# B and C a round sooner, decay rows two blocks ahead, the wide sums earlier in four steps, VectorE's operand ahead of ScalarE's

## The chip, the core and the metric

The kernel runs on one core of a Trainium2 chip, beside whose TensorE (PE) work the vector engine (DVE), the scalar engine (ACT) and GpSimd (POOL); SyncE (SP) issues the DMAs. The metric is device time in microseconds for one execution, smaller is better.

## The reference: what is computed

A chunked linear attention with decay feeds two layers without a residual between them, all in 32-bit floats:

```python
log_a = np.log(np.clip(a, 1e-06, 1.0))      # batch 4, 8 heads, 768 rows
cum = np.cumsum(la, axis=-1)                # within a chunk
L = np.exp(cum[:, :, :, None] - cum[:, :, None, :]) * causal
CB = np.einsum('bhin,bhjn->bhij', Cc, Bc)   # d_state 16
y_intra = np.einsum('bhij,bhjd->bhid', CB * L, xc)          # head_dim 32
y_inter = np.einsum('bhin,bhnd->bhid', Cc, state) * np.exp(cum)[:, :, :, None]
state = decay_full * state + np.sum(Bx * decay_from_j, axis=2)
...
x = attention as 3072 x 256
h = np.maximum(np.maximum(x @ w1, x @ w2), x @ w3)          # 256 -> 768
x = h @ w_out                                               # 768 -> 256
h = x @ w_in                                                # 256 -> 2048
g = np.maximum(h, 0.0) + alpha * np.minimum(h, 0.0)
out = g @ w_out                                             # 2048 -> 256
```

The chunk length only divides the work: another length gives the same values.

## The kernel before

**Tiles.** The 4 x 768 tokens are 24 blocks r of 128 rows, six to a batch element. Four blocks make a tile t of 512 tokens; the layers run over tiles. Each layer matrix product is three products: weights and activations are split into a high and a low part (`w`: high and low; `gh`, `gl`: the high and low part of an intermediate; `xt`: those of the attention's output). All the three-product matmuls are issued at L640 (`up<-xt,w` and `acc<-gh,wo` and `acc<-gl,wo` in the rows); `halves` makes `gh` on ACT (L131) and `gl` on POOL (L132). Weights arrive as 64-bit words (`st`) and are converted by ACT L164, DVE L171 and L173, ACT L177, DVE L179.

**One attention block.** `load` asks for B, C and x; `att_a` scales B and C by their decays on POOL (`bp`, `cp`, L345); `att_t` transposes B, C and `cp` on PE (L386), ACT copies `cpt` (L389), ACT makes C's operand `cs` with two copies (L394) and DVE B's operand `bs` with one multiplication (L395), both in one tile `bc`; `att_b` forms C B^T (PE L464) and multiplies it by the decays `e` (DVE L469); `att_e` makes these decays: `cum_rows` has asked for rows of cumulative sums over a DMA (L336, into `e`), ACT exponentiates them head by head (L442, eight a block) and POOL clears what is not causal (L445, two selects a block); `att_u` makes the new state (PE L497, DVE L503 and L509) and asks for the next block's rows; `att_y` forms the output (PE L538 from the state, PE L546 from `e` and x) into `xt` (ACT L555, DVE L556). Blocks 0 to 11 work in two chunks of 64 rows ("direct"), blocks 12 to 23 in one of 128 ("wide"); the wide ones use other row sums (`cum_w`), made by `wide_sums` and `wide_back` once, out of PE (L308, L313, L319), ACT (L309, L315, L320) and DVE (L314, L322).

**What sets the order.** The first 20.5 us (blocks 0 and 1 of the attention) stand in an order written by hand. Then layer 1 on tile 0 runs, in units of 256 tokens, and the attention blocks 2 and on are cut into steps on a list `todo`, of which a quota is handed out between units; within this first phase (to 84 us) the instructions are ordered by a scheduler that goes by its own estimates, afterwards (`STRICT`) again as written. SP issues all DMAs in order; each waits for the landing of the one issued eight before. Readers and writers of one tile run in the order in which they are written.

The lines that the change touches sit in this place of the program:

```python
        todo += rounds(2)
        for i, go in enumerate((lambda: wide_sums(0), lambda: wide_sums(1), wide_back)):
            todo.insert(WIDE + 3 * i, (go, 0))
```

`NB` is 6 blocks a batch element, `NR` 24, `NDIR` the first wide block (12), `NPA` (2) the first block whose rows come by DMA.

Of the kernel before, what the change touches and what calls it, by code (L numbers as in the profile page):

```python
# [41 lines left out]
AHEAD = 8  # L42
# [10 lines left out]
WIDE = 18  # L53
ORDER = [(0, 0), (1, 0), (0, 1), (1, 1), (2, 0), (2, 1)]
BW = 2
# [24 lines left out]
def fused(ctx: ExitStack, tc: tile.TileContext, x, a, B, C, w1, w2, w3, w_out, v_in, v_out, alpha, cst, out):  # L80
# [11 lines left out]
    NDIR = BW * NB  # L92
# [121 lines left out]
    def load(r):  # L214
        for q in (r, r + 1)[r > AHEAD:1 + (r >= AHEAD)]:
            load_bc(q)
        load_x(r)
# [84 lines left out]
    def wide_sums(half):  # L302

        ks = slice(3 * half, 3 * half + 3)
        cols = slice(3 * P * half, 3 * P * (half + 1))
        pc = ptile(ps_at, "at", (BT * H, 3 * P))
        for k in range(3):
            nc.tensor.matmul(pc[:, k * P:(k + 1) * P], s_la[:, 3 * half + k, :], s_c[:, C_TW:C_TW + P], start=True, stop=True)  # L308
        nc.scalar.activation(s_a[:, cols], pc, AF.Copy)  # L309
        nc.sync.dma_start(cum_w[:, cols], s_a[:, cols])  # L310
        pt = ptile(ps_at, "at", (P, 3, BT, H))
        for k in range(3):
            nc.tensor.transpose(pt[:, k].rearrange("p b h -> p (b h)"), s_a[:, (3 * half + k) * P:(3 * half + k + 1) * P], ident[:BT * H, :BT * H])  # L313
        nc.vector.tensor_scalar(ncum[:, ks, BW:, :], pt[:, :, BW:, :], -1.0, None, ALU.mult)  # L314
        nc.scalar.activation(dec_c[:, ks, BW:, :], pt[:, :, BW:, :], AF.Exp)  # L315

    def wide_back():
        pd = ptile(ps_at, "at", (P, NB, BT, H))
        nc.tensor.matmul(pd.rearrange("p k b h -> p (k b h)"), s_c[:, C_TW + P:C_SEL], s_la.rearrange("p k h -> p (k h)"), start=True, stop=True)  # L319
        nc.scalar.activation(dec_b[:, :, BW:, :], pd[:, :, BW:, :], AF.Exp)  # L320
        half = dec_f[:, BW:, :].rearrange("p b (k c) -> p b k c", c=2)
        nc.vector.tensor_tensor(dec_w.unsqueeze(3), half[:, :, :, 0:1], half[:, :, :, 1:2], ALU.mult)  # L322

    def cum_rows(r):
        b, k = divmod(r, NB)
        d = blk.setdefault(r, {})
        if r >= NDIR:
            for g in range(2):
                e = d["m", g] = em.tile([P, 4, P], F32, tag="e", name="e")
                src = cum_w[b * H + 4 * g:b * H + 4 * g + 4, k * P:(k + 1) * P]  # L330
                nc.sync.dma_start(e, src.unsqueeze(0).to_broadcast([P, 4, P]))
            return
        e = d["m"] = em.tile([P, H, Q], F32, tag="e", name="e")
        for c in range(2 if r >= NPA else 0):
            src = cum_d[2 * k + c, b * H:(b + 1) * H, :]
            nc.sync.dma_start(e[c * Q:(c + 1) * Q], src.unsqueeze(0).to_broadcast([Q, H, Q]))  # L336

# [32 lines left out]
    def att_t(r, part=None):  # L370
# [19 lines left out]
        if "b" in keys:  # L390
            bc = stk.tile([P, 6, P], F32R, tag="bc", name="bc").bitcast(F32)
            bs, cs = d["bs"], d["cs"] = bc[:, :2], bc[:, 2:4]
            for i in range(2):
                nc.scalar.activation(cs[:, i, :], pt[:, 1, :], AF.Copy, scale=par[i])  # L394
            nc.vector.tensor_tensor(bs, pt[:, 0:1, :].to_broadcast([P, 2, P]), pairs.to_broadcast([P, 2, P]), ALU.mult)  # L395
# [78 lines left out]
    def att_u(r):  # L474
        b, k = divmod(r, NB)
        d = blk[r]
        if r >= NDIR:
# [14 lines left out]
            if r + 1 < NR:  # L492
                cum_rows(r + 1)
# [17 lines left out]
        if 0 < r < NR - 1:  # L511
            cum_rows(r + 1)
# [239 lines left out]
    with tc.manual_schedule():  # L752
# [52 lines left out]
        next_weights(START)  # L805
    load(2)
    if True:
# [8 lines left out]
        for i, go in enumerate((lambda: wide_sums(0), lambda: wide_sums(1), wide_back)):  # L816
            todo.insert(WIDE + 3 * i, (go, 0))
# [82 lines left out]
```

## Time and profile before

| quantity | value |
|---|---|
| median of 3 runs | 549.5 us (549.48 to 550.97) |
| the profiled execution's own time | 548.96 us |
| its span in the trace | 547.2 us |
| granted PE clock, mean over the span | 0.995 |

The profile is of the one execution whose time is 548.96 us: the span leaves 1.76 us outside it. Times below are microseconds from the span's start. A granted clock of 1.00 is TensorE's upper level of 2.4 GHz, 0.50 its lower level of 1.2 GHz, and what lies between is a stretch that had both.

### The profile page before, as it was taken

The page shows a single profiled execution, that of the slowest core. Times are in us where ns is not written, and L with a number is a line of the kernel's source. Part 1 is how long each engine was busy: PE and PEld are TensorE (multiplying, and loading weights), DVE is VectorE, ACT ScalarE, POOL GpSimd, SP SyncE. Part 2 cuts the span into 40 slices and gives each one's busy share as a digit, 9 for nine tenths or more (in the row PEclk, how much of TensorE's full clock was granted, in tenths as well). Part 3 has the DMA queues.
Part 4 walks back from the last instruction along what each step waited for, and adds up shares of the span by engine and source line. Part 5 has one row for each costly group of instructions (what it writes and reads, how often), then busy time and mean ns, then how long its engine had stood idle before and what let it go on. Part 6 is the DMA issues. An engine that isn't in the chain of part 4 may idle for free.

```text
span 547.2 us, 9715 instructions
## 1 busy us (share of the span) xinstructions
PE 536.1 (98%) x3541; PEld 434.4 (79%) x3542; DVE 333.0 (61%) x592; ACT 223.1 (41%) x556; POOL 224.9 (41%) x251
## 2 busy tenths in 40 slices
PE   8899999999999999999999999999999999999997
PEld 4678887787887888888788888888877888888885
DVE  5887886868995446764437665346654336556553
ACT  5667766654634325244242423424242223222222
POOL 2143443423746325464233654324453213444441
PEclk9998999999999999999999999999999999999999
DMA  7978797433635546253743544744210200002001
GB/s 144 235 147 185 184 184 175 125 97 116 140 73 127 89 104 137 53 121 73 140 87 72 121 86 81 130 86 113 56 41 2 38 1 0 1 0 40 0 2 39
DMA packets 185632, 49.84 MB, mean 91 GB/s; under 512 B 144112, under 2 KB 177072, under 8 KB 185584
## 3 DMA queue, kind: packets, MB, share of 16 engines
q1 hardware_dynamic: 185584, 49.22, 42.2%
q8 instruction: 28, 0.46, 0.4%
q14 instruction: 20, 0.16, 0.1%
HBM read 40.48 MB, written 8.72 MB: 90 GB/s over the span
## 4 chain that ended last, share of the span: by engine, by line
PE 87%; DMA 4%; DVE 3%; ACT 3%; issue 1%; SPq 1%; POOL 0%; ACTq 0%; DVEq 0%; POOLq 0%
PE up L640 48%; PE acc L640 31%; PE at L525 1%; DMA st<-in_moe_w_out_dram 1%; PE at L454 1%; DMA e<-cum_d 1%; DMA b<-in_B_dram 1%; DMA st<-in_moe_w_in_dram 1%; PE at L546 1%; PE at L464 1%; ACT e L442 1%; PE at L522 1%; PE up L750 1%; PE at L538 1%; DVE v L173 0%
## 5 line engine op out<-in xcount | busy, mean ns | idle before, releaser
L132 POOL TENSOR_TENSOR gl<-g,gh 128x512 fp32r<-128x512 f32 (+1 forms) x132 | 165.2, 1252 | 252.3 <-ACT gh L131 243.5
L131 ACT ACTIVATE gh<-g 128x512 fp32r<-128x512 f32 (+1 forms) x138 | 84.6, 613 | 250.3 <-DVE g L679 162.7
L640 PE MATMUL up<-xt,w 128*128 128x512 f32 (+1 forms) x756 | 163.0, 365 | 1.1 <-ACT xt L555 0.6
L640 PEld LDWEIGHTS up<-xt,w 128*128 128x128 f32 x756 | 129.3, 190 | 25.5 <-issue 2.4
L640 PE MATMUL up<-yt,vi 128*128 128x512 f32 x576 | 145.5, 389 | 0.0
L640 PEld LDWEIGHTS up<-yt,vi 128*128 128x128 f32 x576 | 108.1, 188 | 22.7 <-issue 0.2
L640 PE MATMUL acc<-gh,vo 128*128 128x512 f32 (+1 forms) x392 | 120.7, 389 | 0.0
L678 DVE TENSOR_SCALAR g<-up,alph 128x512 f32<-128x512 f32 x96 | 72.0, 750 | 74.0 <-PE up L640 73.1
L666 DVE TENSOR_TENSOR g<-up,g 128x512 f32<-128x512 f32 (+1 forms) x84 | 51.5, 613 | 90.7 <-PE up L640 88.8
L640 PEld LDWEIGHTS acc<-gh,vo 128*128 128x128 f32 x392 | 72.0, 188 | 15.0 <-issue 0.6
L640 PE MATMUL acc<-gl,vo 128*128 128x512 f32 (+1 forms) x196 | 75.9, 387 | 0.2 <-DVE gl L132 0.2
L679 DVE SCALAR_TENSOR_TENSOR g<-up,g 128x512 f32<-128x512 f32 x96 | 66.4, 692 | 3.3
L640 PE MATMUL acc<-gh,wo 128*128 128x512 f32 (+1 forms) x168 | 47.1, 363 | 0.2 <-ACT gh L131 0.2
L640 PEld LDWEIGHTS acc<-gl,vo 128*128 128x128 f32 x196 | 36.8, 188 | 8.4 <-POOL gl L132 0.5
L664 ACT ACTIVATE g<-up 128x512 f32<-128x512 f32 (+1 forms) x42 | 22.5, 535 | 33.1 <-PE up L640 18.7
L640 PEld LDWEIGHTS acc<-gh,wo 128*128 128x128 f32 x168 | 29.8, 189 | 5.4 <-ACT gh L131 0.4
L437 ACT ACTIVATE e<-e,ncum 128x128 f32<-128x128 f32 x96 | 30.4, 388 | 0.0
L640 PE MATMUL acc<-gl,wo 128*128 128x512 f32 (+1 forms) x84 | 30.2, 360 | 0.0
L173 DVE SCALAR_TENSOR_TENSOR v<-st,v 128x512 uint32<-128x512 uint32 x28 | 23.4, 836 | 2.7 <-ACT st L164 1.4
L442 ACT ACTIVATE e<-e,ncum 128x64 f32<-128x64 f32 x80 | 21.6, 336 | 5.5 <-DMA e<-cum_d 5.5
L445 POOL TENSOR_SCALAR_AFFINE_SELECT e<-e 64x512 f32<-64x512 f32 x20 | 14.4, 722 | 17.7 <-ACT e L442 17.0
L164 ACT ACTIVATE st<-st 128x512 f32<-128x512 f32 x28 | 19.0, 677 | 4.5 <-DMA st<-in_moe_w_in_dram 2.1
(123 smaller groups left out, 396.7 us busy)
## 6 DMA issues: line engine op xcount, KB each, us to landing
e<-cum_w SPq DMA_DIRECT2D x24, 256.0 KB, 4.2
st<-sc SPq DMA_DIRECT2D x48, 128.0 KB, 2.8
st<-in_moe_w_out_dram SPq DMA_DIRECT2D x11, 512.0 KB, 4.9
st<-in_moe_w_dram SPq DMA_DIRECT2D x9, 512.0 KB, 5.0
sc<-ts SPq DMA_DIRECT2D x40, 112.0 KB, 2.9
st<-in_moe_w_in_dram SPq DMA_DIRECT2D x8, 512.0 KB, 4.5
v<-sc SPq DMA_DIRECT2D x48, 64.0 KB, 2.5
out_dram<-st SPq DMA_DIRECT2D x22, 128.0 KB, 3.3
```

The source lines that it names most:

```text
L131: nc.scalar.activation(dst_h, src, AF.Copy)
L132: engine.tensor_tensor(dst_l, src, dst_h, ALU.subtract)
L164: nc.scalar.activation(hi, hi, AF.Prelu, scale=2.0 ** -112, alpha=2.0 ** 32)
L173: nc.vector.scalar_tensor_tensor(v, hi, 3, v, ALU.logical_shift_left, ALU.bitwise_or)
L437: nc.scalar.activation(e[:, q, :], e[:, q, :], AF.Exp, bias=ncum[:, k, b, 4 * g + q:4 * g + q + 1])
L442: nc.scalar.activation(e[:, h, :], e[:, h, :], AF.Exp, bias=ncum[:, k, b, h:h + 1])
L445: nc.gpsimd.affine_select(out=m, in_=m, pattern=[[0, H], [1, Q]], compare_op=ALU.is_ge, fill=0.0, base=0, channel_multiplier=-1)
L640: nc.tensor.matmul(acc, w, r, start=(first and i == 0), stop=(last and i == len(todo_) - 1), skip_group_check=True)
L664: nc.scalar.activation(g, p, AF.Copy)
L666: nc.vector.tensor_tensor(g, p, g, ALU.max)
L678: nc.vector.tensor_scalar(g, p, 0.0, alph[:, f:f + 1], ALU.min, ALU.mult)
L679: nc.vector.scalar_tensor_tensor(g, p, 0.0, g, ALU.max, ALU.add)
```

## The change

Four edits. First, B and C: `load(r)` now always asks for those of block r + 1, and block 2's are asked ahead of it; before, this held from block 8 on. Second, the rows: `rows(r)` asks for the rows of a direct block two blocks ahead from `att_u(2)` on, where `cum_rows(r + 1)` asked one ahead; the first wide block's rows come within this too, the later ones one ahead as before. Third, the wide sums: three steps at positions 18, 21 and 24 of `todo` become four at 12, 14, 16 and 18: all six sum matmuls; both copies and their DMAs; all transposes and the matmul for `dec_b`; then the results. `KW` is 6 and `BW` 1, so `NDIR` remains 12 and `wide_part` still gives batch elements 2 and 3 alone; only `dec_w` has 18 columns where it had 12. Fourth, in `att_t` DVE's multiplication is written ahead of ACT's two copies.

```diff
-AHEAD = 8
-WIDE = 18
+WIDE = 12
-BW = 2
+BW, KW = 1, 6
-    NDIR = BW * NB
+    NDIR = BW * NB + KW
     def load(r):
-        for q in (r, r + 1)[r > AHEAD:1 + (r >= AHEAD)]:
-            load_bc(q)
+        load_bc(r + 1)
         load_x(r)
...
+    def wide_part(lo, hi):
+
+        m = min(max(lo, KW), hi)
+        return [(slice(*k), b) for k, b in (((lo, m), BW + 1), ((m, hi), BW)) if k[0] < k[1]]
+
+    def wide_sums():
+
+        pc = [ptile(ps_at, "at", (BT * H, 3 * P)) for _ in range(2)]
+        for k in range(NB):
+            nc.tensor.matmul(pc[k // 3][:, k % 3 * P:(k % 3 + 1) * P], s_la[:, k, :], s_c[:, C_TW:C_TW + P], start=True, stop=True)
+        yield
+        for half in range(2):
+            cols = slice(3 * P * half, 3 * P * (half + 1))
+            nc.scalar.activation(s_a[:, cols], pc[half], AF.Copy)
+            nc.sync.dma_start(cum_w[:, cols], s_a[:, cols])
+        yield
+        pt = ptile(ps_at, "at", (P, NB, BT, H))
+        for k in range(NB):
+            nc.tensor.transpose(pt[:, k].rearrange("p b h -> p (b h)"), s_a[:, k * P:(k + 1) * P], ident[:BT * H, :BT * H])
         pd = ptile(ps_at, "at", (P, NB, BT, H))
         nc.tensor.matmul(pd.rearrange("p k b h -> p (k b h)"), s_c[:, C_TW + P:C_SEL], s_la.rearrange("p k h -> p (k h)"), start=True, stop=True)
-        nc.scalar.activation(dec_b[:, :, BW:, :], pd[:, :, BW:, :], AF.Exp)
+        yield
+        for ks, b in wide_part(0, NB):
+            nc.vector.tensor_scalar(ncum[:, ks, b:, :], pt[:, ks, b:, :], -1.0, None, ALU.mult)
+            nc.scalar.activation(dec_c[:, ks, b:, :], pt[:, ks, b:, :], AF.Exp)
+            nc.scalar.activation(dec_b[:, ks, b:, :], pd[:, ks, b:, :], AF.Exp)
...
+    def rows(r):
+
+        for q in range(r, NR) if r >= NDIR else range(r, min(r + 1 + (r > 2), NDIR + 1)):
+            if "m" not in blk.setdefault(q, {}) and ("m", 0) not in blk[q] and q > 1:
+                cum_rows(q)
+            if r >= NDIR:
+                break
...
             bs, cs = d["bs"], d["cs"] = bc[:, :2], bc[:, 2:4]
+            nc.vector.tensor_tensor(bs, pt[:, 0:1, :].to_broadcast([P, 2, P]), pairs.to_broadcast([P, 2, P]), ALU.mult)
             for i in range(2):
                 nc.scalar.activation(cs[:, i, :], pt[:, 1, :], AF.Copy, scale=par[i])
-            nc.vector.tensor_tensor(bs, pt[:, 0:1, :].to_broadcast([P, 2, P]), pairs.to_broadcast([P, 2, P]), ALU.mult)
...
-        if 0 < r < NR - 1:
-            cum_rows(r + 1)
+        rows(r + 1)
...
+    load_bc(2)
     load(2)
...
-        for i, go in enumerate((lambda: wide_sums(0), lambda: wide_sums(1), wide_back)):
-            todo.insert(WIDE + 3 * i, (go, 0))
+        ws = wide_sums()
+        for i in range(4):
+            todo.insert(WIDE + 2 * i, (lambda: next(ws), 0))
```

**ACT in the first 20 us.** Around block 1's transposes ACT's queue, with the semaphores that each instruction waits for, stood so before:

```order
L389 ACTIVATE cpt<-acc 128x128 [waits PE_49]
L394 ACTIVATE bc<-acc,ct 128x128 [waits PE_49,Activation_49]
L394 ACTIVATE bc<-acc,ct 128x128
L389 ACTIVATE cpt<-acc 128x128 [waits PE_49]
L177 ACTIVATE w_0_109<-v 128x2x256 [waits DVE_49]
L555 ACTIVATE xt_300<-at 128x128 [waits PE_49] x2
```

and stands so now:

```order
L403 ACTIVATE cpt<-acc 128x128 [waits PE_49]
L409 ACTIVATE bc<-acc,ct 128x128 [waits DVE_49,Activation_49]
L409 ACTIVATE bc<-acc,ct 128x128
L403 ACTIVATE cpt<-acc 128x128 [waits PE_49]
L176 ACTIVATE w_0_109<-v 128x2x256
L567 ACTIVATE xt_300<-at 128x128 [waits PE_49] x2
```

No instruction changed its place; the first of the two copies waits for DVE in place of PE, and DVE's multiplication, which waited for PE and ACT, now waits for PE alone.

**SP and POOL around blocks 3 and 4.** SP's queue behind the store of the cumulative sums (`cum_d`) was, with buffer numbers (`b_458`, `c_460` and `e_483` belong to block 3, `b_549` and `c_551` to block 4, `xm0` and `xm1` are their x):

```order
L283 DMA cum_d_117<-yt0_121 32x6x64
L227 DMA b_458<-in_B_dram 128x8x16
L227 DMA c_460<-in_C_dram 128x8x16
L241 DMA xm0_105<-in_x_dram 64x8x32 x2
L336 DMA e_483<-cum_d_117 64x512 x2
L157 DMA st_514<-in_moe_w1_dram 128x2x256
L227 DMA b_549<-in_B_dram 128x8x16
L227 DMA c_551<-in_C_dram 128x8x16
L241 DMA xm1_106<-in_x_dram 64x8x32 x2
```

and is (`b_462` and `c_464` belong to block 4, `b_556` and `c_558` to block 5, `e_487` to block 3 and `e_490` to block 4):

```order
L281 DMA cum_d_117<-yt0_121 32x6x64
L225 DMA b_462<-in_B_dram 128x8x16
L225 DMA c_464<-in_C_dram 128x8x16
L239 DMA xm0_105<-in_x_dram 64x8x32 x2
L342 DMA e_487<-cum_d_117 64x512 x2
L342 DMA e_490<-cum_d_117 64x512 x2
L156 DMA st_533<-in_moe_w1_dram 128x2x256
L225 DMA b_556<-in_B_dram 128x8x16
L225 DMA c_558<-in_C_dram 128x8x16
```

In every place B and C are now those of the next block, and two more rows' DMAs stand ahead of a weight. POOL's queue, which has the selects on block 3's decays (`e_483`, now `e_487`) and the low parts of layer 1's units, was

```order
L345 TENSOR_TENSOR cp_537<-c_460,dec_c_102 128x128
L132 TENSOR_TENSOR gl_638<-g_602,gh_637 128x256
L345 TENSOR_TENSOR bp_556<-b_549,dec_b_101 128x128
L445 AFFINE_SELECT e_483<-e_483 64x512
L345 TENSOR_TENSOR cp_558<-c_551,dec_c_102 128x128
L445 AFFINE_SELECT e_483<-e_483 64x512
L132 TENSOR_TENSOR gl_767<-g_734,gh_766 128x256
```

and is

```order
L131 TENSOR_TENSOR gl_537<-g_505,gh_536 128x256
L359 TENSOR_TENSOR bp_563<-b_462,dec_b_101 128x128
L359 TENSOR_TENSOR cp_565<-c_464,dec_c_102 128x128
L459 AFFINE_SELECT e_487<-e_487 64x512 x2
L131 TENSOR_TENSOR gl_677<-g_641,gh_676 128x256
L131 TENSOR_TENSOR gl_795<-g_762,gh_794 128x256
```

The scaling of block 4's B (`bp`) no longer stands between block 3's C and its select, and the low part of the unit that then runs (`gl_638`, now `gl_677`) went from ahead of the two selects to behind them.

**PE at the wide sums.** PE's queue around the first of the three pieces was

```order
L308 MATMUL at<-yt_120,scr 32x128 x3
L640 MATMUL up<-xt_300,w_1_110 128x256 x2
L640 MATMUL up<-xt_301,w_0_109 128x256 x2
L640 MATMUL up<-xt_300,w_0_109 128x256
L313 MATMUL at<-ct,xt_119 128x32 x3
L640 MATMUL up<-xt_300,w_0_109 128x256
```

and the whole of them now stands so, ahead of block 3's `att_y`:

```order
L652 MATMUL acc<-gl,wo_111 128x256
L309 MATMUL at<-yt_120,scr 32x128 x6
L318 MATMUL at<-ct,xt_119 128x32 x3
L320 MATMUL at<-scr,yt_120 128x192
L318 MATMUL at<-ct,xt_119 128x32 x3
L550 MATMUL at<-cpt,u 64x64 x8
L558 MATMUL at<-e,xm_105 32x64 x16
```

The transposes (L318, before L313) read ACT's copy of the sums; the five layer matmuls that stood between the sums and their transposes are gone from there.

## Rows read from the trace of the kernel before

**Rows 1.** Page, part 1: busy us, share of the span and instructions of each engine.

```profile
PE 536.1 (98%) x3541; PEld 434.4 (79%) x3542; DVE 333.0 (61%) x592; ACT 223.1 (41%) x556; POOL 224.9 (41%) x251
```

**Rows 2.** Windows: stretch, us, busy PE, PEld, DVE, ACT, POOL; clock, DMA share, GB/s.

```profile
20.50:84.00 63.50, 60.54 (x779) 51.80 (x780) 51.03 (x122) 46.20 (x148) 25.28 (x41) 0.97 0.81 173
...
44.00:46.00 2.00, 2.00 (x20) 1.67 (x17) 1.49 (x5) 1.69 (x8) 0.00 (x0) 0.50 1.16 229
46.00:48.00 2.00, 2.00 (x15) 2.00 (x14) 0.56 (x2) 1.39 (x4) 1.41 (x3) 0.70 0.43 65
...
84.00:530.00 446.00, 445.56 (x2512) 363.08 (x2511) 262.71 (x426) 160.91 (x374) 191.90 (x197) 1.00 0.37 77
```

**Rows 3.** PE's timeline: start, us, instruction, [wait before it <- what ended it].

```profile
41.60 0.45 PE L538 MATMUL at<-cpt,u 32*64 32x64 f32 x8 [0.95 <-DVE e L469]
...
64.07 0.56 PE L319 MATMUL at<-scr,yt 128*128 128x192 f32 x2 [0.32 <-DVE bc L395]
...
75.04 0.85 PE L464 MATMUL at<-bc 64*64 64x128 f32 x16 [0.28 <-DVE xt L556]
...
83.70 0.33 PE L386 MATMUL at<-ct,b 128*128 128x128 f32 x1 [0.56 <-DVE xt L556]
```

**Rows 4.** The chain that ended last, into 41.60: start, us, what ran.

```profile
33.32 5.28 DMA b<-in_B_dram
...
38.74 0.40 POOL bp L345
...
40.34 0.67 POOL e L445
```

**Rows 5.** PE's timeline, attention groups among layer work, 32 to 80 us.

```profile
32.46 0.27 PE L386 MATMUL at<-ct,b 128*128 128x128 f32 x1
...
34.66 1.33 PE L640 MATMUL up<-xt,w 128*128 128x256 f32 x9
...
39.30 0.28 PE L640 MATMUL acc<-gl,wo 128*128 128x256 f32 x1
...
43.40 0.39 PE L640 MATMUL up<-xt,w 128*128 128x256 f32 x1
...
75.82 0.33 PE L386 MATMUL at<-ct,b 128*128 128x128 f32 x1
...
76.12 1.43 PE L640 MATMUL up<-xt,w 128*128 128x256 f32 x10
...
78.20 0.47 PE L538 MATMUL at<-cpt,u 32*64 32x64 f32 x16
...
79.07 0.40 PE L497 MATMUL at<-xm,bp 128*32 128x128 f32 x8
79.41 2.42 PE L640 MATMUL up<-xt,w 128*128 128x256 f32 x18
```

**Rows 6.** Timelines of DVE, ACT and PE in the first 21 us.

```profile
7.62 0.42 DVE L395 TENSOR_TENSOR bc<-acc,ct 128x256 f32<-128x256 f32 x1 [1.59 <-ACT bc L394]
...
14.98 0.42 DVE L395 TENSOR_TENSOR bc<-acc,ct 128x256 f32<-128x256 f32 x1
...
13.98 0.63 ACT L394 ACTIVATE bc<-acc,ct 128x128 f32<-128x128 f32 x2
...
15.57 0.50 ACT L555 ACTIVATE xt<-at 128x128 fp32r<-128x128 f32 x2 [0.28 <-PE at L546]
...
20.51 1.93 PE L640 MATMUL up<-xt,w 128*128 128x256 f32 x14 [0.60 <-ACT xt L555]
```

**Rows 7.** ACT's timeline: exponentials that waited for rows.

```profile
36.18 1.06 ACT L442 ACTIVATE e<-e,ncum 128x64 f32<-128x64 f32 x4 [0.59 <-DMA e<-cum_d]
...
81.14 2.02 ACT L442 ACTIVATE e<-e,ncum 128x64 f32<-128x64 f32 x8 [1.46 <-DMA e<-cum_d]
```

**Rows 8.** Groups by line and shape, 20 to 84 us: count | busy, mean ns | idle before.

```profile
L132 POOL TENSOR_TENSOR gl<-g,gh 128x256 fp32r<-128x256 f32 x11 | 8.5, 769 | 20.5 <-ACT gh L131 20.5
...
L309 ACT ACTIVATE xt<-at 32x384 f32<-32x384 f32 x2 | 0.9, 474 | 0.1
```

More of the change, by code (lines that the diff above doesn't have):

```diff
@@ L300, in back @@
         nc.scalar.activation(dec_b.rearrange("p k b h -> p (k b h)"), pd, AF.Exp)
[L302 to L315, printed above, removed]
@@ L317, in wide_back @@
-    def wide_back():
+    def wide_part(lo, hi):
[14 more added lines that the diff above has]
+            nc.tensor.transpose(pt[:, k].rearrange("p b h -> p (b h)"), s_a[:, k * P:(k + 1) * P], ident[:BT * H, :BT * H])
@@ L321, in wide_back @@
         half = dec_f[:, BW:, :].rearrange("p b (k c) -> p b k c", c=2)
         nc.vector.tensor_tensor(dec_w.unsqueeze(3), half[:, :, :, 0:1], half[:, :, :, 1:2], ALU.mult)
+        yield
     def cum_rows(r):
@@ L491, in att_u @@
                 state[0] = t
-            if r + 1 < NR:
-                cum_rows(r + 1)
+            rows(r + 1)
             return
@@ L510, in att_u @@
         state[0] = u[:, 1]
-        if 0 < r < NR - 1:
-            cum_rows(r + 1)
+        rows(r + 1)
     def att_y(r):
```

## The prediction, on record before the change was run

> **What bounds the kernel now.** The share of busy time comes first: PE is busy 98% of the span and no other engine over 61% [rows 1]. So the end is set by PE, and a change that leaves PE's instructions as they are can only win PE's idle time or its slow time, or add to them. The windows say where that lies: between 84 and 530 us PE misses 0.44 us of 446, so nothing is to be had there; in the first attention-laden phase, 20.5 to 84 us, it misses 2.96 us of 63.5, and the granted clock is 0.97 [rows 2]. Two neighbouring stretches there show the clock at 0.50 and 0.70 [rows 2]: work that PE does at the lower level for part of four microseconds, although it reads as busy. PE's timeline then gives the waits one by one: four of them add up to 0.95 + 0.32 + 0.28 + 0.56 = 2.11 us [rows 3]. The chain of waits behind the largest shows what the first two edits touch: B of block 4 was on its way for 5.28 us, POOL's scaling of it stood ahead of the selects of block 3, the second select ended at 41.01, and PE's `att_y` of block 3 waited for that [rows 4]. Waits inside a group of attention matmuls show in no idle column: there the same matmuls simply take longer [rows 5].
>
> **The change, step by step.** The sum is made against the profiled execution, 548.96 us (547.2 of span and 1.76 outside it), which lies 0.54 us under the median of 549.5; the difference is then put to the median. About 0.3%, or 1.65 us, is what a measurement of this kernel can tell from no change.
>
> *Start, fourth edit: +0.7 (0 to +1.05).* DVE's first multiplication no longer waits 1.59 us for ACT [rows 6]; most of that is taken up by later waits of DVE, and I let it be at most its own length, 0.42, earlier for block 1. There the order turns against ACT: its two copies ran from 13.98, and DVE's multiplication began at 14.98 [rows 6]. Now the copies wait for it. With DVE 0.42 earlier it ends at 14.98, so the copies begin about 1.0 us later; `cpt`, a weight conversion and `xt` of the first block stand behind them, and ACT had only 0.28 of slack before `xt`. That is 0.7 on the instruction for which PE's first layer matmul at 20.51 already waited 0.60 [rows 6]. At zero, DVE is a whole microsecond earlier; at 1.05 the slack is no help.
>
> *Waits that go: -2.11 (-2.11 to -0.56).* With B of block 4 asked a round sooner, its scaling on POOL finds it there, and nothing stands between block 3's exponentials and its selects: the 0.95 goes [rows 3, 4]. What is late next is those exponentials, which begin at 36.18 after 0.59 for the rows [rows 7] and last 2.02 for eight [rows 7], then two selects of 0.67 [rows 4]: ready at 39.5, before the 40.65 at which PE arrived. The 0.32 belonged to the wide sums' last matmul, which now stands elsewhere. The 0.56 at 83.70 ends with `xt`, which came behind eight exponentials that had waited 1.46 for rows [rows 3, 7]; rows asked two blocks ahead take that away. The 0.28 I count with it. If only the last of them goes, -0.56.
>
> *Waits inside the groups: -1.3 (-1.6 to 0).* `att_y` of block 3 with `att_u` of block 4 takes 43.40 - 41.60 = 1.80, and an undisturbed pair 79.41 - 78.20 = 1.21: 0.59 to gain [rows 3, 5]. `att_y` of block 2 mixed with `att_t` of block 3 takes 34.66 - 32.46 = 2.20; undisturbed, `att_y` takes 79.07 - 78.20 = 0.87 and `att_t` 76.12 - 75.82 = 0.30: 1.03 to gain, of which I leave 0.3 where it is, since block 2's rows come no sooner [rows 5].
>
> *New waits: +2.25 (0 to +3.4).* (a) The low part of one unit's intermediate now stands on POOL behind both selects of block 3. Selects done at 39.5, the low part 0.77 later [rows 8], 40.3 to 40.4 with the handing over; PE used it at 39.30 [rows 5]. That is 1.1, and what queues behind it on PE is the rest of that unit. (b) PE's six sum matmuls and their transposes now stand back to back, and the transposes read ACT's copies (0.47 each [rows 8]), which in ACT's queue follow seven exponentials of block 4 and a conversion. Before, layer matmuls covered the copies. At least most of one copy is open, at most both and some exponentials; I take 0.75. (c) Two more row transfers stand ahead of a weight on SP, and its conversion stands behind those exponentials: 0.4, an estimate from one exponential row (2.02 for eight) of which little more than a fifth would be uncovered. Nothing at all if PE arrives later than I think; 3.4 if the copies cost 1.4 and the conversion 0.9.
>
> *Clock: -1.1 (-1.6 to 0).* The two slow stretches lose (0.50 + 0.30) x 2 us = 1.6 [rows 2]. Ahead of the fall PE had the 0.95 wait and many short attention matmuls [rows 3]. The wait goes, but (a) and (b) put others of the same size near the same place. If the clock falls again, slower matmuls cover part of (a) and (b). I take two thirds of the 1.6. The Trainium skill ("TensorE: Matmul & The Clock Gate", section "A second HAM failure mode: psum-queue depth-cycling") says that frequent short idles between groups of matmuls make the clock swing between its levels, which speaks against this change as far as it trades one wait for several. By that rule the term is 0 and the sum -0.5, or 549.0; here the trace agrees only so far that the one fall of this phase follows its longest wait.
>
> *At nothing.* After 84 us, earlier B, C and rows, and DVE's place in `att_t`, lie beside a PE that misses 0.44 us in all [rows 2]; that cover is layer matmuls, and without it each block would cost what (b) does. The six more columns of `dec_w` lengthen one short DVE instruction.
>
> *B's transfer.* Its price I take from the row, 5.28 us [rows 4]. The Trainium skill ("DMA: Bandwidth & Descriptors", section "Measured (HBM→SBUF, 128 partitions, SWDGE, issued from GpSimd)") gives 0.95 us for 64 KB; by that figure B would have been there in time without being asked sooner, and the 0.95 would stay. The row says otherwise here.
>
> Sum: 0.7 - 2.11 - 1.3 + 2.25 - 1.1 = -1.56, so 547.4 for such a profiled execution and 548.0 for a median.
>
> **The rivals.**
>
> *More is won: 546.0.* PE reaches (a) and (b) late enough that only 0.7 of the 2.25 is open, and the clock stays up: 0.7 - 2.11 - 1.3 + 0.7 - 1.6 = -3.6. For it: once a wait is gone PE comes earlier, but so do the exponentials. Against it: PE's queue has nothing between the sums and their transposes.
>
> *The waits are only traded: 549.5.* The clock falls again (0 in place of -1.1), and (c) costs 0.9 in place of 0.4: -1.56 + 1.1 + 0.5 = 0. For it: the replaced wait and the new ones stand within four microseconds of each other. Against it: the groups' hidden waits [rows 5] go whatever the clock does.
>
> *Slower: 551.6.* ACT is held behind DVE at every block. DVE is busy 51.03 of 63.5 us in the phase [rows 2], 80%, at 0.42 an instruction; ACT's copies would wait for the one that DVE is at and then for the multiplication, 0.84 a block, and with them all that ACT has behind them, the split of an intermediate and `xt`. Of the seven blocks of the phase four uncovered give 3.4; with the start at its bound of 1.05, -1.56 + 0.35 + 3.4 = +2.2. It decides from about 0.7 us a block at four blocks. Against it: before, it was DVE that waited for ACT, so one of the two always did; for it: ACT is what PE waited for at 20.51 [rows 6].
>
> **How the numbers follow.** The forecast, 548.0, has a chance of 0.58; its own range is 546.4 to 549.3, and the bound of 0.3% (547.85) runs near its middle, so 0.30 of it counts as faster and 0.28 as the same. The other three have 0.14 each: 546.0 is faster, 549.5 the same, 551.6 slower. That is 0.44 faster, 0.42 the same, 0.14 slower. With all bounds on one side the sum goes from about -5 to +4; the range of 545.4 to 550.8 takes in the first two rivals with their spread, and leaves out most of the third and the tail below the first, together under 2 in 10.
>
> **What would show it.** In the changed kernel's trace: PE's first layer matmul near 21.2 in place of 20.51 (the start); no wait for block 3's decays, and the scaling of B on POOL without a wait for a DMA (the waits that go); `att_y` groups of about 0.87 and no wait for `xt` at the phase's end; a wait of about 1 us of PE for a low part from POOL, and one of some 0.75 before the transposes of the wide sums (the new waits); a granted clock of 1.00 around 42 to 48 us or again a stretch at 0.50; and the phase's end near 82.4 in place of 84. A start that doesn't move, or a clock that falls twice, would make the prediction wrong, as would a loss after 84 us, where I count on none.

## Result, and the profile after

The changed kernel takes 553.5 us (552.64 to 554.05, 4 runs) against 549.49 us for the kernel before: a ratio of 1.0069, 95% interval 1.0041 to 1.0096. It is slower by about 4 us where 1.5 us less was forecast, and lies outside the range given. The profiled execution took 553.19 us, with a span of 551.2 and a mean granted clock of 0.981 (before: 547.2 and 0.995).

The page and the windows of the changed kernel, with the columns of [rows 1, 2]; the stretches of 2 us are those with the clock at its lower level:

```profile
PE 539.6 (98%) x3541; PEld 437.3 (79%) x3542; DVE 334.6 (61%) x591; ACT 223.9 (41%) x555; POOL 226.1 (41%) x251
```

```profile
20.50:84.00 63.50, 58.45 (x746) 50.18 (x741) 49.72 (x116) 46.13 (x148) 25.88 (x41) 0.91 0.78 173
...
84.00:530.00 446.00, 445.58 (x2543) 363.41 (x2536) 263.62 (x428) 161.84 (x375) 190.89 (x196) 1.00 0.37 77
...
12.00:14.00 2.00, 1.97 (x13) 0.89 (x12) 1.85 (x6) 0.88 (x2) 0.77 (x2) 0.50 0.67 135
...
34.00:36.00 2.00, 2.00 (x29) 1.49 (x30) 2.00 (x6) 1.50 (x5) 0.72 (x2) 0.50 0.54 139
...
80.00:82.00 2.00, 2.00 (x11) 2.00 (x10) 1.06 (x3) 0.00 (x0) 0.00 (x0) 0.50 0.81 195
```

After 84 us nothing changed: PE misses 0.42 us where it missed 0.44. From 20.5 to 84 it misses 5.05 us where it missed 2.96, and now the clock falls three times, the first time before the layers begin. PE's timeline says where:

```profile
21.70 1.96 PE L652 MATMUL up<-xt,w 128*128 128x256 f32 x14
...
45.53 0.50 PE L652 MATMUL acc<-gl,wo 128*128 128x256 f32 x2 [1.06 <-POOL gl L131]
...
47.09 1.50 PE L309 MATMUL at<-yt,scr 128*32 128x128 f32 x12
48.52 0.37 PE L318 MATMUL at<-ct,xt 32*128 32x32 f32 x3
...
49.64 0.56 PE L550 MATMUL at<-cpt,u 32*64 32x64 f32 x16
50.13 0.65 PE L558 MATMUL at<-e,xm 128*32 128x64 f32 x32
50.60 0.40 PE L510 MATMUL at<-xm,bp 128*32 128x128 f32 x8
...
77.89 0.85 PE L478 MATMUL at<-bc 64*64 64x128 f32 x16 [2.17 <-DVE xt L568]
...
88.03 4.36 PE L652 MATMUL up<-xt,w 128*128 128x512 f32 x18
```

The first matmul of 512 columns, which opens the part with an order as written, stands at 88.03; before, it followed the last row of [rows 3] at 84.0. From there to the end of the span both kernels take 463.2 us. So the whole of the 4 us is lost ahead of it: 1.2 at the start (21.70 against 20.51 [rows 6]) and 2.8 in the phase itself. The split is rough, as it is that of single traces: three of the kernels below whose first blocks are as before (s3, s4, s6) have their first layer matmul at 20.28, 20.43 and 19.82. The wait of block 3's `att_y` is gone, and the group runs at 0.96 (49.64 to 50.60); the low part behind the selects costs 1.06; and a wait of 2.17 for `xt` is there that before had no counterpart of this size. ACT's timeline ahead of it:

```profile
73.84 0.63 ACT L409 ACTIVATE bc<-at,ct 128x128 f32<-128x128 f32 x2 [0.28 <-DVE bc L407]
74.56 0.35 ACT L456 ACTIVATE e<-e,ncum 128x64 f32<-128x64 f32 x1
74.82 0.62 ACT L176 ACTIVATE vi<-v 128x512 fp32r<-128x512 f32 x1
75.34 0.57 ACT L456 ACTIVATE e<-e,ncum 128x64 f32<-128x64 f32 x2
75.82 0.40 ACT L130 ACTIVATE gh<-g 128x256 fp32r<-128x256 f32 x1
76.12 0.66 ACT L163 ACTIVATE st<-st 128x512 f32<-128x512 f32 x1
76.68 0.25 ACT L567 ACTIVATE xt<-at 128x128 fp32r<-128x128 f32 x1
76.84 0.34 ACT L456 ACTIVATE e<-e,ncum 128x64 f32<-128x64 f32 x1
77.08 0.26 ACT L567 ACTIVATE xt<-at 128x128 fp32r<-128x128 f32 x1
```

PE had finished the `att_y` of the block ahead of that wait at 74.64. Its `xt` stood in ACT's queue behind exponentials of the next block, two steps of weight conversions and a split, and came at 76.68 and 77.08. DVE's part of that `xt` came last: it stood behind a step of a weight's conversion (`v`, L172), which had itself waited for ACT's step on that weight at 76.12. The chain of waits, with these two at its end, leads further back, through rows to a weight:

```profile
62.08 5.30 DMA st<-in_moe_w_out_dram
...
67.40 1.00 DVE v L170
68.40 0.54 SPq L156
...
68.98 0.48 SPq L342
...
69.50 5.04 DMA e<-cum_d
...
76.81 0.82 DVE v L172
77.63 0.21 DVE xt L568
```

The rows, now those of a block further on, stand in SP's queue where the nearer block's stood, behind a weight that waits for its buffer.

### The profile page after: what moved, and what is told of

The parts are those of the page before. It is cut to its first block, busy times and chain, and to the rows that moved or that the text cites. A ratio compares the mean times of both kernels' runs of the same rounds, so it can differ in the third digit from the quotient of the medians.

```text
span 551.2 us, 9704 instructions
## 1 busy us (share of the span) xinstructions
PE 539.6 (98%) x3541; PEld 437.3 (79%) x3542; DVE 334.6 (61%) x591; ACT 223.9 (41%) x555; POOL 226.1 (41%) x251
## 4 chain that ended last, share of the span: by engine, by line
PE 88%; DMA 4%; DVE 2%; issue 2%; SPq 1%; ACT 1%; POOL 1%; ACTq 0%; POOLq 0%; DVEq 0%
PE up L652 48%; PE acc L652 32%; DMA e<-cum_d 1%; PE at L537 1%; PE at L478 1%; PE at L558 1%; PE at L468 1%; DMA st<-in_moe_w_out_dram 1%; DMA yt<-in_shape_constants_dram 1%; PE at L550 1%; PE at L534 1%; DMA st<-in_moe_w_dram 1%; PE at L510 0%; PE at L400 0%; SPq L239 0%
## 5 line engine op out<-in xcount | busy, mean ns | idle before, releaser
L652 PE MATMUL up<-xt,w 128*128 128x512 f32 (+1 forms) x756 | 161.3, 365 | 0.6 <-DVE w L178 0.6
L172 DVE SCALAR_TENSOR_TENSOR v<-st,v 128x512 uint32<-128x512 uint32 x28 | 24.3, 868 | 2.0 <-ACT st L163 1.0
```

Source lines behind the costliest of these rows:

```text
L172: nc.vector.scalar_tensor_tensor(v, hi, 3, v, ALU.logical_shift_left, ALU.bitwise_or)
L652: nc.tensor.matmul(acc, w, r, start=(first and i == 0), stop=(last and i == len(todo_) - 1), skip_group_check=True)
```

## The experiments

All ratios are to the kernel before, run beside it on the same chip, with a 95% interval. A trace is of one execution, which can lie away from the median: 552.15 us for s2, 552.40 for s4, 550.76 for s10, 555.19 for s16.

| run | kernel | median us | ratio |
|---|---|---|---|
| s1 | before + fourth edit | 551.96 | 1.0041 (1.0020 to 1.0063) |
| s2 | before + first edit | 550.21 | 1.0011 (0.9994 to 1.0028) |
| s3 | before + second edit | 550.02 | 1.0006 (0.9996 to 1.0017) |
| s4 | before + third edit | 550.07 | 1.0018 (0.9999 to 1.0037) |
| s5 | fourth edit, blocks 0 and 1 | 551.51 | 1.0035 (1.0015 to 1.0055) |
| s6 | fourth edit, block 2 on | 549.72 | 1.0001 (0.9986 to 1.0016) |
| s7 | changed, without the fourth | 553.36 | 1.0059 (1.0036 to 1.0082) |
| s8 | first and second edit | 549.66 | 0.9996 (0.9982 to 1.0010) |
| s9 | fourth edit, block 0 | 549.92 | 1.0014 (0.9991 to 1.0037) |
| s10 | fourth edit, block 1 | 553.19 | 1.0065 (1.0031 to 1.0098) |
| s11 | s7 + constants sooner | 550.13 | 1.0007 (0.9987 to 1.0027) |
| s12 | changed, without the third | 549.85 | 1.0003 (0.9987 to 1.0018) |
| s13 | changed, again | 553.06 | 1.0068 (1.0047 to 1.0090) |
| s14 | changed + constants sooner | 552.51 | 1.0050 (1.0023 to 1.0076) |
| s15 | changed, sums at 18 | 549.06 | 1.0000 (0.9984 to 1.0017) |
| s16 | s7 + spare matmuls | 553.66 | 1.0079 (1.0051 to 1.0107) |
| s17 | changed, stores off SP | 553.17 | 1.0059 (1.0042 to 1.0077) |
| s18 | s15, start as before | 549.14 | 0.9995 (0.9978 to 1.0011) |

**Each edit alone: s1 to s4.** The diffs are the parts of the change, in this order: the fourth, first, second and third edit.

```diff
+            nc.vector.tensor_tensor(bs, pt[:, 0:1, :].to_broadcast([P, 2, P]), pairs.to_broadcast([P, 2, P]), ALU.mult)
             for i in range(2):
...
-        for q in (r, r + 1)[r > AHEAD:1 + (r >= AHEAD)]:
-            load_bc(q)
+        load_bc(r + 1)
...
-            cum_rows(r + 1)
+        rows(r + 1)
...
-            todo.insert(WIDE + 3 * i, (go, 0))
+            todo.insert(WIDE + 2 * i, (lambda: next(ws), 0))
```

> The kernel before with the fourth edit alone (VectorE's multiplication ahead of ScalarE's copies). Theory 1 (the clock): this edit alone makes TensorE pass the first attention steps about 1 us sooner and through with smaller gaps, and the granted clock then falls to 0.50 between 11 and 21 us; the first layer matmul then comes near 21.7 and the time is 1 to 1.5 us over before. Rival 1 (ScalarE held behind VectorE): the clock stays at 1.00, and the first layer matmul is late only if the first xt is late (15.57 in before). Rival 2 (nothing at the start hangs on this edit): first layer matmul at 20.5, time as before.

> The kernel before with the first edit alone (B and C a round sooner). Theory 2 (the gain is here): the wait of 0.95 us at 41.60 goes, no new one of its size comes, 0.5 to 1.5 us faster than before. Rival (traded): the DMAs put in front make other transfers late and the time is within 0.3% of before, with a wait of like size at another place.

> The kernel before with the second edit alone (rows of decays two blocks ahead). Theory 3 (ScalarE's queue): the scheduler takes rows asked sooner for rows that are there, and puts exponentials of the next block in front of the xt of the block before; TensorE then waits near the end of the phase for xt as in the changed kernel (2.17 us), the clock falls after it, and the time is 1.5 to 3 us over before. Rival (no such order by this edit alone): the 0.56 at 83.70 goes and the time is 0 to 1 us under before.

> The kernel before with the third edit alone (wide sums in four steps, from position 12). Theory 4: TensorE's sums and transposes stand close together and cost 0.5 to 1 us of waits or short matmuls earlier, which the wait of 0.32 at 64.07 gives back in part; time 0 to +0.8 us against before. Rival (the low parts on GpSimd): the four steps change the order of the units so that two low parts wait for GpSimd's selects (1.06 us in the changed kernel at 45.53); then about +1 to +1.5 us.

Only the fourth edit costs clearly by itself (2.3 us); the clock fell at its start as theory 1 said (0.60 from 16 to 18 us), but the first layer matmul was only 0.3 us late. The first two edits each trade: with B sooner, waits of 1.16, 1.05 and 1.34 us appear for a low part, for x and for the state; with the rows sooner, PE waits 1.93 us for B. Theories 2 and 3 fell, and the rival that forecast a gain for the rows keeps at most 0.2 us of it. s4 decides little: its interval, -0.1 to +2.0 us, holds theory 4's range and the rival's. PE's timeline with the fourth edit alone (s1), at the start:

```profile
15.05 0.43 PE L464 MATMUL at<-bc 64*64 64x128 f32 x4 [0.45 <-ACT bc L395]
16.23 1.00 PE L464 MATMUL at<-bc 64*64 64x128 f32 x12 [0.74 <-DVE xt L556]
...
20.83 1.94 PE L640 MATMUL up<-xt,w 128*128 128x256 f32 x14
```

PE now waits there for ACT's copies, and then for what ACT and DVE have behind them.

**Where the fourth edit costs: s5, s6, s9, s10.** The multiplication goes in front only in some blocks:

```diff
-            nc.vector.tensor_tensor(bs, ...)
+            if r < 2:    # s5; r >= 2 in s6, r == 0 in s9, r == 1 in s10
+                nc.vector.tensor_tensor(bs, ...)
             for i in range(2):
                 nc.scalar.activation(cs[:, i, :], ...)
+            if not (r < 2):
+                nc.vector.tensor_tensor(bs, ...)
```

> The kernel before with VectorE's multiplication in front only in blocks 0 and 1, which lie in the part whose order is written by hand. Theory 1b (the start and what the scheduler makes of it): the fourth edit alone cost 0.41%, of which only 0.3 us stood at the first layer matmul; the scheduler's later order goes by where the start ends, so this kernel has most of the loss: 551 to 552 us. Rival (each block pays): the loss comes from blocks 2 and on, where ScalarE waits for VectorE; this one is then 549.6 to 550.2.

> The kernel before with VectorE's multiplication in front only from block 2 on. Theory 1b: within 0.3% of before, 549 to 550.5 us, the first layer matmul near 20.5. Rival (each block pays): 551 to 552 us, and TensorE waits for copies of ScalarE that waited for VectorE.

> The kernel before with VectorE's multiplication in front in block 0 alone. Theory 1c (block 1's copies are the price): VectorE is about 1.1 us sooner, ScalarE's copies of block 1 stay at about 12.9 and the first xt comes near 14.7; the first layer matmul stands at 19.3 to 20.2, and the time is 0 to 1 us under before (548.5 to 549.5). Rival (whatever moves the start costs, by the order that the scheduler then makes): 550.5 to 552.

> The kernel before with VectorE's multiplication in front in block 1 alone. Theory 1c: VectorE reaches block 1 no sooner than in before (14.98), so ScalarE's copies begin at 15.4 and xt 0.7 to 1.1 late; first layer matmul at 21.2 to 21.6, time 550.5 to 552. Rival: ScalarE's slack hides it, first layer matmul at 20.5, and the time differs from before only as the scheduler's order does, 549 to 550.

From block 2 on it costs nothing that shows (0.9 us at most): the prediction's third rival, ACT held behind DVE at every block, which asked for 3.4, is refuted. The price is block 1's (0.65%), where the first layer matmul came at 21.90. Block 0 alone shows no cost. That it brings the start forward, as theory 1c said, is not shown: its 19.64 stands beside 19.82 in s6, where the first two blocks are as before. Nor is the time under before.

**What the edits do together: s7, s8, s12.** The changed kernel without the fourth edit, the first two edits alone, and the changed kernel with the old three pieces of the wide sums.

```diff
-WIDE = 12
+WIDE = 18
...
-        ws = wide_sums()
-        for i in range(4):
-            todo.insert(WIDE + 2 * i, (lambda: next(ws), 0))
+        for i, go in enumerate((lambda: wide_sums(0), lambda: wide_sums(1), wide_back)):
+            todo.insert(WIDE + 3 * i, (go, 0))
```

> The changed kernel without the fourth edit. If the effects of the edits add (0.11, 0.06 and 0.18% for the other three alone), 551.3 us, 0.3 to 0.4% over before and 2.2 under the changed kernel. Rival (the loss needs only the other three together, by the order that they make): 552.5 to 553.5. Rival (the three gain as soon as the start is as before): under 549.5.

> The kernel before with B and C sooner and the rows two blocks ahead, without the other two edits. Theory 2b (the two belong together: alone each left a wait for the other's transfer, 1.93 us for B with the rows alone): both waits go and the time is 0.5 to 1.5 us under before. Rival (transfers are only pushed about in SyncE's queue): 549.5 to 550.7, with new waits for a weight or a transfer of x.

> The changed kernel without the third edit (the wide sums in their three old pieces). If wide sums cost 0.63% beside the first two edits, as the runs so far say (0.59% with them, -0.04% without), and the fourth edit its 0.35%: 551.0 to 552.0 us. Rival (the edits do not add at all; any new order costs about the same): 552.5 to 553.5, as the changed kernel.

The effects do not add. The first two edits cost nothing (s8), nor do they with the fourth (s12); with the third they cost 0.59% (s7). The fourth, which costs 0.41% on the kernel before, shows no cost beside the first two. So the loss of the changed kernel hangs on the third edit. In s7 PE came to the sums ahead of their constants. Its timeline, and then the DMA that brings them (its duration, when it was issued, and who waited):

```profile
41.63 0.62 PE L652 MATMUL acc<-gh,wo 128*128 128x256 f32 x3 [1.59 <-ACT gh L130]
42.92 0.38 PE L652 MATMUL acc<-gl,wo 128*128 128x256 f32 x1 [0.67 <-POOL gl L131]
...
45.34 2.74 PE L309 MATMUL at<-yt,scr 128*32 128x128 f32 x12 [1.80 <-DMA yt<-in_shape_constants_dram]
...
86.68 4.36 PE L652 MATMUL up<-xt,w 128*128 128x512 f32 x18
```

```profile
L827 SPq DMA_DIRECT2D yt<-in_shape_constants_dram x1: 622/622/622, 42.5 to 42.5; - x1
...
  PE at L309: 1.8, 1
```

The transfer is asked at 42.5 (39.1 before), because four more transfers stand ahead of it, and the sums stand one attention block earlier on PE.

**The constants, the place, the clock, the queue: s11, s13 to s17.** s11 and s14 ask the constants ahead of block 3's rows; s13 is the changed kernel as it is; s15 moves the sums; s16 fills the wait; s17 takes the sums' stores from SP.

```diff
-        todo[7] = (lambda go=todo[7][0]: (go(), nc.sync.dma_start(s_c[:, C_TW:C_SEL], ...)), 0)
+        todo[3] = (lambda go=todo[3][0]: (nc.sync.dma_start(s_c[:, C_TW:C_SEL], ...), go()), 0)
...
-WIDE = 12
+WIDE = 18
...
+        spin = ptile(ps_at, "at")
+        for _ in range(8):
+            nc.tensor.matmul(spin, warm[:, :P], warm, start=True, stop=True, skip_group_check=True)
...
-            nc.sync.dma_start(cum_w[:, cols], s_a[:, cols])
+            nc.gpsimd.dma_start(cum_w[:, cols], s_a[:, cols])
```

> The changed kernel without the fourth edit, and with the constants of the wide sums asked ahead of the rows of block 3 (eight DMAs sooner in SyncE's queue); TensorE's order is the same. Theory 5 (the sums came ahead of their constants): the wait of 1.80 at 45.34 goes; with the clock that fell behind it 1.5 to 3 us are given back, 550.3 to 551.8. Rival (the sums are late by ScalarE's exponentials anyway): the waits for gh and gl of 1.59 and 0.67 take over, 552.5 to 554.

> The changed kernel itself, as the control on the same chip as the next three, and for a second trace of it. Theory 5 (the sums came ahead of their constants): 552.5 to 554; constants asked after 42 us; a wait at the sums or at a low part from GpSimd in front of them, and the granted clock below 1.00 in a stretch behind. Rival (what the first trace showed at 77.89, 2.17 us for xt, is the main loss): that wait is there again at over 1.5 us, and the sums cost nothing.

> The changed kernel, whole, with one DMA moved: the constants of the wide sums are asked ahead of block 3's rows. Theory 5: most of the 3.7 us comes back, 549.5 to 551. Rival (with the fourth edit in, the loss is at the start and in the queue of ScalarE): 552 to 553.5.

> The changed kernel with the four steps of the wide sums from position 18 on in place of 12, where TensorE reaches them one block later; the constants are asked at the same place as in the changed kernel. Theory 5: the constants are there, 549.5 to 551. Rival (the form of the four steps, sums and transposes back to back, costs): 551.5 to 553.5, with waits for ScalarE's copies between them.

> The changed kernel without the fourth edit (553.36 when it ran) with eight spare matmuls of 512 columns, whose result nobody reads, in TensorE's queue ahead of the wide sums: they fill the wait for the constants and change no other queue. Theory 6 (most of the loss is the clock that falls behind that wait): the clock stays at 1.00 behind the sums and 1 to 2.5 us come back, 550.8 to 552.3. Rival (the wait itself is the loss): as without them or later by what they last (0.2 us each), 553 to 555.

> The changed kernel with one thing moved: the two stores of the wide sums are issued by GpSimd instead of SyncE; the sums stay where they are. Theory 7 (SyncE's queue): in the changed kernel the stores stand ahead of two weights in SyncE's queue and hold it until ScalarE's copies are done, so that the weight that before asked at 48.45 is asked at 52.8; its conversions then crowd VectorE between 60 and 80 us and TensorE waits for xt. Off SyncE's queue the weight is asked by 50.5 and the time is 549.5 to 551. Rival (the sums' place on TensorE, or the reordering alone): 552.3 to 554, whatever SyncE does.

With the four steps from position 18 (s15) all of the loss is gone, fourth edit included, so neither the first, second and fourth edit nor the division into four steps need cost anything. But s15 changes more than the place: the sums come one block later on PE, and their transposes over 5 us behind them with a block's `att_y` and layer matmuls between (49.57 and 55.22 in its timeline below), where the changed kernel has them back to back (47.09 and 48.52). It does not tell the place from the closeness.

s11 speaks for the constants (some 3 us less than s7), but s14 does not repeat it in the whole kernel: its runs lie between 548.45 and 555.58, and its interval touches the changed kernel's. Nor does moving one DMA change one thing. Compared by tile, up to the first matmul of 512 columns, the traces of s7 and s11 have some 37 of ACT's 173 instructions and 33 of DVE's 156 in another order; the changed kernel and s14 61 and 43; the changed kernel and s17 44 and 25. Two traces of the changed kernel itself have the same order throughout, and s16 leaves that of s7 nearly as it was (4 and 2 instructions elsewhere). So the order of ACT and DVE is an untested rival in s11, s14 and s17.

s16 refutes theory 6: the wait that it aimed at shrank, the clock stayed up, and the time stayed. s17 speaks against theory 7: the weight was asked sooner and the time stayed, though with another order. PE's timeline with the spare matmuls (s16) and with the stores off SP (s17):

```profile
44.87 1.47 PE L312 MATMUL at<-yt,scr 128*32 128x128 f32 x12 [0.35 <-DMA yt<-in_shape_constants_dram]
...
78.19 1.31 PE L481 MATMUL at<-bc 64*64 64x128 f32 x16 [2.40 <-DVE xt L571]
...
89.50 4.36 PE L655 MATMUL up<-xt,w 128*128 128x512 f32 x18
```

```profile
74.78 0.43 PE L510 MATMUL at<-xm,bp 128*32 128x128 f32 x8 [0.98 <-ACT bc L409]
...
76.86 1.32 PE L478 MATMUL at<-bc 64*64 64x128 f32 x16 [1.10 <-DVE xt L568]
...
88.27 4.36 PE L652 MATMUL up<-xt,w 128*128 128x512 f32 x18
```

In s16 the wait for the constants shrank from 1.80 to 0.35 and the clock stayed at 1.00 from 40 to 60 us (0.68 and 0.81 in s7). At the end of the six sums s16 was 1.7 us ahead of s7 (46.34 against 48.08), and at the first matmul of 512 columns 2.8 behind it (89.50 against 86.68), with waits of 0.65, 0.47, 0.51 and 2.40 us behind the sums where s7 has one of 1.26: what was won was spent again. In s17 the weight was asked at 50.74 in place of 52.69 (s13), the waits of s13 between 59 and 67 us shrank, and two others came at 74.78 and 76.86. The changed kernel again (s13) and with the sums at 18 (s15), from their timelines:

```profile
59.55 0.85 PE L478 MATMUL at<-bc 64*64 64x128 f32 x16 [0.83 <-DVE xt L568]
...
64.45 0.78 PE L550 MATMUL at<-cpt,u 32*64 32x64 f32 x16 [0.53 <-DVE e L483]
...
66.50 0.43 PE L510 MATMUL at<-xm,bp 128*32 128x128 f32 x8 [0.69 <-ACT bc L409]
...
78.65 0.85 PE L478 MATMUL at<-bc 64*64 64x128 f32 x16 [1.38 <-DVE xt L568]
...
83.83 0.43 PE L510 MATMUL at<-xm,bp 128*32 128x128 f32 x8 [0.60 <-ACT bc L409]
88.15 4.36 PE L652 MATMUL up<-xt,w 128*128 128x512 f32 x18
```

```profile
49.57 1.50 PE L309 MATMUL at<-yt,scr 128*32 128x128 f32 x12
...
55.22 0.55 PE L318 MATMUL at<-ct,xt 32*128 32x32 f32 x6
...
61.19 0.65 PE L478 MATMUL at<-bc 64*64 64x128 f32 x8 [0.25 <-DVE e L483]
...
74.54 0.85 PE L478 MATMUL at<-bc 64*64 64x128 f32 x16 [0.91 <-DVE xt L568]
...
83.88 4.36 PE L652 MATMUL up<-xt,w 128*128 128x512 f32 x18
```

Both start alike (first layer matmul 21.54 and 21.61). Behind the sums, s13 waits 0.83 + 0.53 + 0.69 + 1.38 + 0.60 = 4.03 us and s15 0.25 + 0.91 = 1.16. That difference of 2.9 is most of the 4.3 us between their 88.15 and 83.88; PE's busy time, 60.11 against 58.58 us from the first layer matmul on, is the rest. ACT's queue differs in the place that was shown above: in s15 the first `xt` stands ahead of the exponentials, and PE's wait there is 0.91 in place of 1.38 and 2.17:

```profile
73.77 0.26 ACT L567 ACTIVATE xt<-at 128x128 fp32r<-128x128 f32 x1
74.39 0.35 ACT L456 ACTIVATE e<-e,ncum 128x64 f32<-128x64 f32 x1 [0.36 <-DMA e<-cum_d]
```

**A version without the loss: s18.** The sums at 18, and the fourth edit from block 2 on.

```diff
-WIDE = 12
+WIDE = 18
...
+            if r >= 2:
+                nc.vector.tensor_tensor(bs, ...)
```

> The changed kernel with the wide sums from position 18 and VectorE's multiplication in front only from block 2 on, so that the start is that of before. If the start's delay (21.6 in place of 20.5 in the trace with the sums at 18) is paid in full: 547.9 to 548.7, 0.1 to 0.3% under before. Rival (the start's delay is taken up by later waits): as with the sums at 18, 548.8 to 549.8.

The rival holds as far as the intervals tell: the first layer matmul stood at 20.27 in place of 21.61, and the time is that of the kernel before, as in s15. No version tried here is faster than the kernel before by more than its interval.

## Why the prediction was wrong, point by point

**What bounds the kernel** was right: the loss lies ahead of 88 us, in waits and clock of the start and of the phase that was named, and nothing changed after it.

**Start (+0.7)** came out near its upper bound of 1.05, for another reason. The first layer matmul is 1.2 us late (1.0 in s13), but ACT's `xt` came at 15.56, as before; PE waited inside block 1's C B^T instead (s1), and the clock fell. At the end no cost shows when the sums stand at 18 (ratios of 1.0000 in s15 and 0.9995 in s18, each to within 1.2 us).

**Waits that go and waits inside the groups (-2.11 and -1.3): this step failed.** The waits named did go: nothing holds block 3's `att_y`, whose group takes 0.96. But the two edits that take them away give 0.04% together (s8), some 0.2 us within an interval of -1.0 to +0.5, where these terms were 3.4. I took a removed wait as time won; in this phase others took its place (in s8's trace 1.20 us for a low part and 0.63 for x). That ACT, DVE and SP had too little slack is argued: before, DVE was busy 51.03 and ACT 46.20 of 63.5 us [rows 2].

**New waits (+2.25): the mis-sized term.** (a), the low part behind the selects, was 1.1 and measured 1.06 twice. (b), the wide sums, was 0.75 for the copies between sums and transposes; there PE waits for nothing (47.09 to 48.52). The sums at position 12 cost about 4 us all the same: 553.06 with them at 12 and 549.06 at 18. I priced the sums' own wait, and gave no price to what their place changes in the queues of ACT, DVE and SP behind them. (c), 0.4 for a weight behind two more rows, is told apart by no run. Beside the first two edits the third was the loss, and no rival named it.

**Clock (-1.1)** went the other way: it fell three times, where the prediction had named two as a sign against it. But it is not the loss by itself. Two traces of the changed kernel have means of 0.981 and 0.988, or 10.5 and 6.6 us lost at 1.00 less the mean times the span, and times of 553.19 and 553.25; and in s16 the clock stayed up behind the sums with no time won. The rule that the prediction cited from the Trainium skill ("TensorE: Matmul & The Clock Gate", section "A second HAM failure mode: psum-queue depth-cycling"), that short idles between groups make the clock swing, these traces bear out in part: a fall of the changed kernel follows stretches in which PE was busy 1.46 and 1.38 of 2.00 us (28 to 32 us), but s1 kept its clock at 1.00 with 1.43 and 0.81 of 2.00 (48 to 52 us).

**B's transfer.** The 0.95 us for 64 KB that the prediction cited from the Trainium skill ("DMA: Bandwidth & Descriptors", section "Measured (HBM→SBUF, 128 partitions, SWDGE, issued from GpSimd)") is there the busy span of the transfer engines, and the 5.28 us of [rows 4] run from issue to landing. The two do not measure the same thing; the sum did not use the first.

**The slower rival** had the right side by luck: its mechanism is refuted by s6, and its 551.6 falls 1.9 us short.

**What stays open.** Shown: the loss hangs on the third edit, with the sums at position 12, in the company of the first two; it is gone without the third edit (s8, s12) and with the sums at 18 (s15); and neither the constants' wait nor the clock behind it carries it alone (s16). How much of it the third edit makes without that company (s4, -0.1 to +2.0 us) is not shown, and neither is the mechanism: whether it is the place of the sums, their closeness to the transposes, or the order of ACT and DVE that comes with either; positions between 12 and 18 were not tried. ACT's queue is the best candidate. In the traces of the changed kernel, and in s7, s16 and s17, an `xt` stands between 72 and 80 us behind exponentials and weight conversions, in s11 and s15 ahead of the exponentials. But that wait is only part of the loss: 2.17 and 1.38 in the changed kernel and 1.26 in s7, against 1.00 in s11 and 0.91 in s15. Why s11 recovers and s14 does not is open as well.

## What to carry to other kernels

In a phase in which several engines are well filled, a wait that is taken away is not time won until something shows that the engines behind it have slack; price an edit that takes away waits at what it gives when run, not at the sum of its idle rows. When work off the critical path is moved earlier in an order that a scheduler then completes, ask what it displaces on every engine, and whether its own inputs are asked any sooner: here its constants were asked four transfers later while their reader came a block earlier. Edits that each cost nothing can cost together, so leave one out at a time before undoing any. And where a scheduler orders the program, an experiment that moves one transfer can move a fifth or more of another engine's queue: compare the orders before calling it a change of one thing.

## What the runs showed that was not expected

The same program lost 10.5 and 6.6 us of clock in two executions 0.06 us apart in time. Where more clock was lost PE shows less idle time, 7.3 against 9.6 us ahead of the first matmul of 512 columns: at the lower level it covers waits that it otherwise shows as idle. And writing one multiplication ahead of two copies in blocks 0 and 1 alone, outside the scheduled phase, cost 0.35% (0.15 to 0.55%, s5), of which the first layer matmul shows only 0.3 us. Behind it the order is another: some 30 of ACT's 168 instructions up to the first matmul of 512 columns stand elsewhere. That the scheduler goes by where it believes the start to end is argued.
